# The last head's way to the output: normalised by two transposes, projected with the last tile

## Chip, core and metric

The kernel runs on one NeuronCore of a Trainium2 chip. The metric is the device time of one execution in microseconds (us). The engines are TensorE (PE in the profile; its weight loads are PEld), VectorE (DVE), ScalarE (ACT), GpSimd (POOL) and SyncE (SP, which here only issues DMAs).

## The reference

Two attention blocks of 32 heads with 18 columns each run over the same 2048 rows of `x` (576 columns), and a gate mixes them row by row:

```python
g = sigmoid((x * gate_w).sum(-1, keepdims=True))
a = A(x)    # o = softmax(q k^T / sqrt(18)) v, each head with its own k and v; then o @ A_wo
b = B(x)    # the same, but all heads share one k and one v; then o @ B_wo
return g * a + (1 - g) * b
```

`A_wo` and `B_wo` are 576 x 576. The kernel treats the job as 64 heads: 0 to 31 are those of B, 32 to 63 those of A. Their outputs, scaled by the gate and by one over the softmax sum, stand one below the other as 1152 rows, and the result is one product of these rows, transposed, with the 1152 rows of both output matrices.

## The kernel before

A first stage (lines 95 to 434) projects `x`. Then one loop (from line 799) goes through 1024 steps, 16 for each of the 64 heads, two at a time; T counts steps, a pass of the loop is a pair. In a step, TensorE makes the scores of 128 keys against all 2048 queries (`step_scores`, L550, four matmuls), ACT takes four exponentials (L557), and TensorE adds the product with the values into `acc`, one PSUM bank that holds a head's sum (`step_pv`, L563). 22 steps ahead, `step_max` finds row maxima for a later head: matmuls L513, reductions on VectorE L522 and L519, one relu per pair on ACT, L516.

The order within a pair is written out by hand in strings (lines 791 to 797). UNIT is used in a pair that has an output unit, PLAIN in one that has none, END and AFTER around a head's end, ALONE from T = 1002, when no maxima are left to find. `s` is a score, `m` a maximum, `P`, `Q`, `h`, `H` and the like products with the values (P and Q whole, h and H half the columns), `U` an output unit.

When a head is done, `head_out` copies `acc` to SBUF (L573) and DMAs its 18 rows into a tile `ot` of 128 rows, and its softmax sums to DRAM. When the 128 rows of a tile are complete, `normalise` loads the sums and the gate, takes the reciprocal times the gate (L601, L602), writes it to DRAM, reads it back spread over rows as `R`, multiplies, and splits the result into a high and a low float32r part. It is a generator; the list `slow` holds such generators, and the loop takes one step of it per pair (two where T > 1000, none where (T + 22) is a multiple of 16).

The output projection (`out_proj`) goes in three segments of the 1152 rows: tiles 0 to 3, tiles 4 to 7, and tile 8. Each has 32 units (16 row blocks of the output times two halves of 288 columns). A unit is three matmuls for each tile (high times high, and the two mixed products; L679) and one addition into `oacc` on VectorE (L687). So a unit of the second segment has 12 matmuls, one of the third 3. `SEG` (line 771) gives for each segment when its weights are prepared, and between which steps its units are due: 942 to 1008 for the second, 1021 to 1034 for the third, so that 12 units of the third run in the loop and the other 20 behind it.

Tile 8 holds rows 1024 to 1151. Its first 110 belong to heads 56 to 62. They are normalised at T = 1010 at once (`run(normalise(8, at_end=True))`, multiplications and splits on VectorE, L619, L123, L125), into two tiles `end` that stay in SBUF. The last 18 rows belong to head 63, which is done only when the loop ends. `last_out` treats it by itself: it copies `acc` (L708), splits it (L121, L125), stacks high, high and low parts by 12 DMAs into `stk`, and gets the 2048 factors as columns `rl` by four transposes (L720), a reciprocal (L722) and a product with the gate (L724). The remaining units of the third segment run; then 32 matmuls with 54 rows (L730) multiply the stack with the last 18 rows of the weights (high, low, high), and VectorE scales each by `rl` and adds it to `oacc` (L733). After both halves of a row block SP stores its 288 KB.

PSUM has eight banks here: three `ps`, four `pm` and `acc`.

Of the kernel before, what the change touches and what calls it, by code (L numbers as in the profile page):

```python
# [14 lines left out]
OP = mybir.AluOpType  # L15
# [34 lines left out]
def gated_mix_kernel(ctx: ExitStack, tc: tile.TileContext, xT, wall, wv, wo, out):  # L50
# [3 lines left out]
    def dma(o, i, eng=None):  # L54
        o, i = (x.bitcast(F32) if x.dtype == F32R else x for x in (o, i))
        return (eng or nc.sync).dma_start(o, i)  # L56
# [62 lines left out]
    def split(src, h, l, eng_h, eng_l):  # L119
        if eng_h is nc.scalar:  # L120
            nc.scalar.activation(h, src, AF.Copy)  # L121
        else:
            eng_h.tensor_copy(h, src)  # L123
        if l is not None:
            eng_l.tensor_tensor(l, src, h.bitcast(F32), op=OP.subtract)  # L125
# [463 lines left out]
    def normalise(t, at_end=False):  # L589

        u0 = 0 if t == 0 else last_head(t - 1) + 1
        u1 = min(last_head(t) + 1, NU - 1)
        rows = min(P, DH * (NU - 1) - P * t)
        n = (u1 - u0) * 16
        sm = L["work"].tile([P, P], F32, name="sm", bufs=1)
        dma(sm[:n, :], sum_d[u0:u1, :].rearrange("h (s f) -> (h s) f", f=P))
        gt = L["work"].tile([P, P], F32, name="gt", bufs=1)
        dma(gt[:n, :], gu_d[u0:u1, :].rearrange("h (s f) -> (h s) f", f=P))
        yield
        yield  # L600
        nc.vector.reciprocal(sm[:n, :], sm[:n, :])  # L601
# [12 lines left out]
        yield  # L614
        if at_end:
            L["end"] = {y: L["pool"].tile([P, S], F32R, name=f"end{y}") for y in "hl"}
            for c in range(4):
                cs = slice(512 * c, 512 * c + 512)
                nc.vector.tensor_tensor(ot[:rows, cs], ot[:rows, cs], R[:rows, cs], op=OP.mult)  # L619
                split(ot[:rows, cs], L["end"]["h"][:rows, cs], L["end"]["l"][:rows, cs], nc.vector, nc.vector)  # L620
            return
        for c in range(4):
            cs = slice(512 * c, 512 * c + 512)
            h = L["work"].tile([P, 512], F32R, name="oh", bufs=1)
            l = L["work"].tile([P, 512], F32R, name="ol", bufs=1)
            nc.gpsimd.tensor_tensor(ot[:rows, cs], ot[:rows, cs], R[:rows, cs], op=OP.mult)
            yield
            split(ot[:rows, cs], h[:rows], l[:rows], nc.gpsimd, nc.gpsimd)
            yield
            yield  # L630
            dma(on_d[0][P * t:P * t + rows, cs], h[:rows])
            dma(on_d[1][P * t:P * t + rows, cs], l[:rows])
            yield
# [15 lines left out]
    def out_proj(t0, rows, first=False):  # L649

        nt = len(rows)
        oacc = L["oacc"]
        O = {}

        def load(q):
            for x, y in enumerate("hl"):
                if "end" in L:
                    O[q, y] = L["end"][y][:, 256 * q:256 * q + 256].rearrange("p (t s) -> p t s", t=1)
                    continue
                t = L["pool"].tile([P, nt, 256], F32R, name=f"oi{y}", bufs=2)  # L660
                dma(t, on_d[x][P * t0:P * (t0 + nt), 256 * q:256 * q + 256]
                    .rearrange("(t p) s -> p t s", p=P))
                O[q, y] = t

        load(0)
        yield
        w = WO[t0]
        for q in range(8):
            if q < 7:
                load(q + 1)  # L670
            o = {y: O[q, y] for y in "hl"}
            for s2 in range(2):
                st_ = 2 * q + s2
                for hf in range(2):
                    fp = ps_m.tile([P, 512], F32, name="pm")
                    n = 0
                    for a, b in PRODS:
                        for t, r in enumerate(rows):
                            nc.tensor.matmul(fp[:, 0:288], o[b][:r, t, s2 * P:(s2 + 1) * P],  # L679
                                             w[a][:r, t, 288 * hf:288 * hf + 288],  # L680
                                             start=(n == 0), stop=(n == 3 * nt - 1))
                            n += 1
                    dst = oacc[:, st_, 288 * hf:288 * hf + 288]
                    if first:
                        nc.scalar.activation(dst, fp[:, 0:288], AF.Copy)
                    else:
                        nc.vector.tensor_tensor(dst, fp[:, 0:288], dst, op=OP.add)  # L687
                    yield


    def prep_last():
        p2 = L["pool"]
        r0 = DH * (NU - 1)
        st = p2.tile([64, D], F32, name="wlst", tag="wost")
        L["wl"] = p2.tile([64, D], F32R, name="wl")
        l = p2.tile([64, D], F32R, name="wll", tag="wlst2")
        for i in range(3):
            dma(st[18 * i:18 * i + 18, :], wo[r0:r0 + 18, :])
        L["g"] = p2.tile([P, 16], F32, name="gl")
        dma(L["g"], g_d[1].rearrange("(s p) -> p s", p=P))  # L700
        yield
        split(st[:54], L["wl"][:54], l[:54], nc.gpsimd, nc.gpsimd)
        yield
        dma(L["wl"][18:36, :], l[18:36, :])

    def last_out():
        oe = L["work"].tile([P, 512], F32, name="oe", bufs=1)
        nc.scalar.activation(oe, acc, AF.Copy)  # L708
        oh = L["work"].tile([P, 512], F32R, name="oh", bufs=1)
        ol = L["work"].tile([P, 512], F32R, name="ol", bufs=1)  # L710
        split(oe, oh, ol, nc.scalar, nc.vector)
        stk = L["pool"].tile([64, S], F32R, name="stk")
        for j in range(4):
            cs = slice(512 * j, 512 * j + 512)
            dma(stk[0:18, cs], oh[32 * j:32 * j + 18, :])
            dma(stk[18:36, cs], oh[32 * j:32 * j + 18, :])
            dma(stk[36:54, cs], ol[32 * j:32 * j + 18, :])
        pt = ps_m.tile([P, 512], F32, name="pm")
        for c in range(4):
            nc.tensor.transpose(pt[:, P * c:P * c + P], oe[:, P * c:P * c + P], ident)  # L720
        r = L["work"].tile([P, 16], F32, name="rl")
        nc.vector.reciprocal(r.rearrange("p (j c) -> p c j", c=4),  # L722
                             pt.rearrange("p (c j d) -> p c j d", c=4, d=32)[:, :, :, 18])
        nc.vector.tensor_tensor(r, r, L["g"], op=OP.mult)  # L724
        oacc = L["oacc"]
        yield
        for st_ in range(16):
            for hf in range(2):
                ps = ps_m.tile([P, 512], F32, name="pm")
                nc.tensor.matmul(ps[:, 0:288], stk[0:54, st_ * P:st_ * P + P],  # L730
                                 L["wl"][0:54, 288 * hf:288 * hf + 288], start=True, stop=True)
                dst = oacc[:, st_, 288 * hf:288 * hf + 288]
                nc.vector.scalar_tensor_tensor(dst, ps[:, 0:288], r[:, st_:st_ + 1], dst,  # L733
                                               op0=OP.mult, op1=OP.add)
            dma(out[st_ * P:(st_ + 1) * P, :], oacc[:, st_, :])


    NSTEP = 16 * NU
# [28 lines left out]
    slow = [gates()]  # L767
    for t in range(8):
        when(16 * (last_head(t) + 1) + 3, lambda t=t: slow.append(normalise(t)))
    when(16 * (NU - 1) + 2, lambda: run(normalise(8, at_end=True)))  # L770
    SEG = ((0, [P] * 4, 450, 521, 857), (4, [P] * 4, 862, 942, 1008), (8, [DH * (NU - 1) - 8 * P], 950, 1021, 1034))
    for t0, rows, Ta, Tb, Tc in SEG:
        when(Ta, lambda t0=t0, rows=rows: slow.append(prep_wo(t0, rows)))
        when(Tb - 4, lambda t0=t0, rows=rows: (todo.append(out_proj(t0, rows, first=t0 == 0)), pull(1)))
    when(980, lambda: slow.append(prep_last()))


# [63 lines left out]
                        slow.pop(0)  # L841
    while slow:
        run(slow.pop(0))
    tail = last_out()
    next(tail)
    pull(10 ** 9)
    run(tail)


# [32 lines left out]
```

## Time and profile before

| | |
|---|---|
| median of 3 runs | 2694.31 us (2694.18 to 2694.47) |
| the profiled execution | 2694.18 us |
| its span (first to last instruction) | 2692.4 us |
| TensorE busy | 2658.4 us, 99% |
| VectorE busy | 2428.6 us, 90% |
| ACT busy | 2389.0 us, 89% |
| mean granted TensorE clock | 0.997 |

Busy time counts overlapping instructions of an engine once. Matmuls are pipelined and their ends are modelled, so a busy TensorE is not one at its peak. In lists of instructions the first number is the start in us from the span's start, the second the length of the stretch, then engine, line, operation, output and inputs, shapes and the count; in brackets stands how long the engine had been idle before and what ended it. The chain of waits is followed back from the last instruction; each of its lines is a start, a length and what the end waited for there.

### The profile page before, as it was taken

The numbers are of one execution on the slowest core, as the hardware profiler recorded it, in microseconds if no ns is written. First come the engines' busy times: TensorE is split into PE (matmuls) and PEld (weight loads), VectorE is DVE, ScalarE is ACT, GpSimd is POOL, SyncE is SP. The second block draws the span as 40 slices with busy tenths as digits, with TensorE's granted clock in tenths as the row PEclk, the third lists the DMA queues.
The fourth block names the chain that finished last, engine by engine and source line by source line (L and its number), as shares of the span: only waits on it lengthen the run. The fifth ranks groups of instructions, "written<-read, shape, count | busy, mean of one in ns | idle before, by whom it ended". The sixth has DMA issues, their size and how long they took to land.

```text
span 2692.4 us, 57950 instructions
## 1 busy us (share of the span) xinstructions
PE 2658.4 (99%) x22210; PEld 956.5 (36%) x22210; DVE 2428.6 (90%) x4616; ACT 2389.0 (89%) x4810; POOL 280.1 (10%) x520
## 2 busy tenths in 40 slices
PE   9999999999999999999999999999999999999999
PEld 6878322222222222222223333333333332223444
DVE  8347999999999999999999999999999999998865
ACT  4341899999999999999999999999999999998875
POOL 4740000002001100100110002000200011011000
PEclk9999999999999999999999999999999999999998
DMA  6332000011001100210132112112121212122312
GB/s 200 124 111 76 23 20 20 20 34 42 28 17 46 44 20 18 53 32 20 36 76 82 51 43 85 42 50 65 55 67 50 59 50 60 39 76 81 88 36 96
DMA packets 127089, 150.36 MB, mean 56 GB/s; under 512 B 55339, under 2 KB 94411, under 8 KB 125614
## 3 DMA queue, kind: packets, MB, share of 16 engines
q1 hardware_dynamic: 113628, 121.86, 16.0%
q0 software_dynamic: 7968, 19.23, 2.1%
q10 hardware_dynamic: 5216, 5.57, 0.6%
q8 instruction: 174, 2.85, 0.4%
q14 instruction: 103, 0.84, 0.1%
HBM read 90.89 MB, written 46.45 MB: 51 GB/s over the span
## 4 chain that ended last, share of the span: by engine, by line
ACT 53%; PE 35%; DVE 6%; DMA 2%; issue 2%; SPq 1%; POOL 0%; DVEq 0%; ACTq 0%; POOLq 0%
ACT pt L557 47%; PE acc L563 12%; PE ps L550 11%; ACT xb L516 6%; PE pm L679 4%; DVE mx L522 3%; PE pm L243 3%; PE ps L243 2%; PE ps L292 2%; PE pm L513 1%; SPq L56 1%; DVE oe L573 1%; DVE junk L519 1%; DMA oih<-onh 1%; DMA R<-r_d 1%
## 5 line engine op out<-in xcount | busy, mean ns | idle before, releaser
L557 ACT ACTIVATE pt<-ps 128x512 f32<-128x512 f32 x4052 | 2093.8, 639 | 64.6 <-PE pm L513 57.9
L522 DVE TENSOR_REDUCE mx<-pm 128x1 f32<-128x512 f32 x3094 | 1939.1, 682 | 86.9 <-PE pm L513 71.1
L550 PE MATMUL ps<-qs,ksb 56*128 56x512 f16 x2688 | 816.6, 379 | 12.0 <-ACT pt L557 0.6
L513 PE MATMUL pm<-ksb,qs 54*128 54x512 f16 x2363 | 737.2, 382 | 1.2 <-DVE mx L522 0.4
L563 PE MATMUL acc<-pt,vb 128*19 128x512 f32 (+1 forms) x6136 | 591.3, 457 | 1.9
L563 PE MATMUL acc<-pt,vg 128*19 128x256 f32 (+1 forms) x5664 | 579.5, 481 | 2.3 <-DVE oe L573 0.5
L513 PEld LDWEIGHTS <-qs 54*128 54x128 f16 x4096 | 330.5, 93 | 252.1 <-issue 195.3
L550 PE MATMUL ps<-qs,ksa 56*128 56x512 f16 x1364 | 404.4, 379 | 4.8 <-ACT pt L557 1.3
L550 PEld LDWEIGHTS <-ksb 56*128 56x128 f16 x2688 | 174.9, 94 | 616.2 <-issue 569.9
L513 PE MATMUL pm<-ksa,qs 54*128 54x512 f16 x1232 | 384.8, 382 | 0.6 <-ACT xb L516 0.4
L519 DVE CUSTOM_DVE_ANT_0 junk<-pm,xb 128x512 bf16<-128x512 f32 x501 | 340.5, 680 | 0.1
L516 ACT ACTIVATE xb<-pm 128x512 f32<-128x512 f32 x501 | 318.2, 635 | 0.4 <-PE pm L513 0.4
L550 PEld LDWEIGHTS <-ksa 56*128 56x128 f16 x1408 | 89.3, 94 | 328.8 <-issue 297.7
L532 POOL TENSOR_SCALAR mt<-mt 128x32 f32<-128x32 f32 x64 | 18.5, 288 | 1606.2 <-DVE mt L530 1606.2
L563 PEld LDWEIGHTS acc<-pt,vb 128*19 128x19 f32 x6136 | 103.9, 96 | 221.7 <-issue 204.6
L563 PEld LDWEIGHTS acc<-pt,vg 128*19 128x19 f32 x5664 | 96.0, 97 | 222.9 <-issue 205.0
L513 PE MATMUL pm<-kdb,qs 54*128 54x512 f16 x373 | 141.7, 380 | 0.0
L573 DVE COPY oe<-acc 128x512 f32<-128x512 f32 x63 | 43.6, 692 | 30.0 <-PE acc L563 26.9
L295 ACT ACTIVATE vst<-ps 128x288 f32<-128x288 f32 x32 | 13.1, 411 | 62.9 <-PE ps L292 62.9
L251 ACT ACTIVATE ph<-ps,tv 128x512 f16<-128x512 f32 x29 | 19.8, 686 | 50.4 <-PE ps L243 34.3
L251 ACT ACTIVATE ph<-pm,tv 128x512 f16<-128x512 f32 x27 | 18.4, 686 | 48.4 <-PE pm L243 35.7
L257 DVE SCALAR_TENSOR_TENSOR pl<-pm,tv,ph 128x512 f16<-128x512 f32 x27 | 20.1, 749 | 37.9 <-ACT ph L251 24.9
(150 smaller groups left out, 1505.5 us busy)
## 6 DMA issues: line engine op xcount, KB each, us to landing
qs<-qkh SPq DMA_DIRECT2D x244, 72.0 KB
qs<-qkl SPq DMA_DIRECT2D x122, 72.0 KB
onh<-oh SPq DMA_DIRECT2D x32, 256.0 KB
onl<-ol SPq DMA_DIRECT2D x32, 256.0 KB
oih<-onh SPq DMA_DIRECT2D x16, 512.0 KB
oil<-onl SPq DMA_DIRECT2D x16, 512.0 KB
ot<-oe SPq DMA_DIRECT2D x220, 36.0 KB
R<-r_d SPq DMA_DIRECT2D x55, 144.0 KB
```

Of the source, the lines that this page charges most:

```text
L243: nc.tensor.matmul(fp[:, a0:b0], w[a][:kr, k, :], X[b][:kr, k, s0 + a0:s0 + b0], start=(n == 0), stop=(n == len(PROJ) - 1), skip_group_che ...
L251: nc.scalar.activation(h, fp, AF.Copy, scale=t)
L292: nc.tensor.matmul(fp[:, 0:288], X[b][:kr, k, st_ * P:(st_ + 1) * P], w[a][:kr, k, :], start=(n == 0), stop=(n == len(PROJ) - 1))
L513: nc.tensor.matmul(pm, qs[u % 3][b:b + 54, i * P:(i + 1) * P], k, start=True, stop=True)
L516: nc.scalar.activation(MX["x", u, i], pm, AF.Relu)
L519: nc.vector.tensor_tensor_reduce(junk, pm, MX.pop(("x", u, i)), 1.0, -3e38, op0=OP.add, op1=OP.max, accum_out=MX[u][:, i, c:c + 1])
L522: nc.vector.tensor_reduce(MX[u][:, i, c:c + 1], pm, axis=AX.X, op=OP.max)
L550: nc.tensor.matmul(ps, kst(u)[b:b + 56, i * P:(i + 1) * P], qs[u % 3][b:b + 56, c * 512:(c + 1) * 512], start=True, stop=True)
L557: nc.scalar.activation(pt, ps, AF.Exp, scale=SCALE / LIFT ** 2)
L563: nc.tensor.matmul(acc[32 * j:32 * j + 19, a:b], v_of(u, i), PT[u, i, j][:, a:b], start=(i == 0 and a == 0), stop=(i == 15), skip_group_ch ...
L573: nc.vector.tensor_copy(oe, acc)
L679: nc.tensor.matmul(fp[:, 0:288], o[b][:r, t, s2 * P:(s2 + 1) * P], w[a][:r, t, 288 * hf:288 * hf + 288], start=(n == 0), stop=(n == 3 * nt ...
```

## The change

- The last head is normalised in SBUF. `acc` is copied by two engines, ACT the left half of its columns, VectorE the right. Four transposes turn it, VectorE takes the reciprocals, multiplies with the gate, and multiplies the turned head with the factors (a product of 512 columns, read from PSUM). Four transposes turn it back; ACT and VectorE split it; eight DMAs, four from SP and four from ACT, put the 18 rows under the 110 in the `end` tiles.
- Tile 8 is then projected with 128 rows: 32 units of three matmuls, all behind the loop, and a plain addition. The third segment's units are gone from the loop, and so are the 54-row matmuls, their 12 DMAs and their weights. The units use seven PSUM banks, and the stores are issued by SP and ACT in turn.
- Five idle matmuls (54 rows, 512 columns, into `acc`) stand between the two groups of transposes, 14 behind the second.
- The first 110 rows are normalised through `slow`, with one more stop ahead of each of the four column blocks.
- The second segment's units are due until step 1016 instead of 1008.

```diff
             for c in range(4):
                 cs = slice(512 * c, 512 * c + 512)
+                yield
                 nc.vector.tensor_tensor(ot[:rows, cs], ot[:rows, cs], R[:rows, cs], op=OP.mult)
...
+    def end_bank(n=[0]):
+        n[0] += 1
+        return ps_s.tile([P, 512], F32, name="ps") if n[0] % 7 < 3 else ps_m.tile([P, 512], F32, name="pm")
...
+        def idle(n):
+            for _ in range(n):
+                nc.tensor.matmul(acc, qs[0][0:54, 0:P], qs[0][0:54, 0:512], start=True, stop=True)
+
+        nc.scalar.activation(oe[:, 0:256], acc[:, 0:256], AF.Copy)
+        nc.vector.tensor_copy(oe[:, 256:512], acc[:, 256:512])
+        pt, pb = end_bank(), end_bank()
         for c in range(4):
             nc.tensor.transpose(pt[:, P * c:P * c + P], oe[:, P * c:P * c + P], ident)
+        idle(5)
...
+        nc.vector.reciprocal(r.rearrange("p (j c) -> p c j", c=4), p4[:, :, :, DH])
         nc.vector.tensor_tensor(r, r, L["g"], op=OP.mult)
+        nc.vector.tensor_tensor(o4, p4, r.rearrange("p (j c) -> p c j", c=4).unsqueeze(3).to_broadcast([P, 4, 4, 32]),
+                                op=OP.mult)
+        for c in range(4):
+            nc.tensor.transpose(pb[:, P * c:P * c + P], ot[:, P * c:P * c + P], ident)
+        idle(14)
+        nc.scalar.activation(oh, pb, AF.Copy)
+        nc.vector.tensor_tensor(ol, pb, oh.bitcast(F32), op=OP.subtract)
+        r0 = DH * (NU - 1) - 8 * P
+        for j in range(4):
+            dma(end["h"][r0:P, 512 * j:512 * j + 512], oh[32 * j:32 * j + DH, :])
+            dma(end["l"][r0:P, 512 * j:512 * j + 512], ol[32 * j:32 * j + DH, :], nc.scalar)
+        w = WO[8]
         for st_ in range(16):
             for hf in range(2):
+                fp = end_bank()
+                for n, (a, b) in enumerate(PRODS):
+                    nc.tensor.matmul(fp[:, 0:288], end[b][:, st_ * P:(st_ + 1) * P],
+                                     w[a][:, 0, 288 * hf:288 * hf + 288], start=(n == 0), stop=(n == 2))
+                dst = L["oacc"][:, st_, 288 * hf:288 * hf + 288]
+                nc.vector.tensor_tensor(dst, fp[:, 0:288], dst, op=OP.add)
+            dma(out[st_ * P:(st_ + 1) * P, :], L["oacc"][:, st_, :], nc.scalar if st_ % 2 else None)
...
-    when(16 * (NU - 1) + 2, lambda: run(normalise(8, at_end=True)))
-    SEG = ((0, [P] * 4, 450, 521, 857), (4, [P] * 4, 862, 942, 1008), (8, [DH * (NU - 1) - 8 * P], 950, 1021, 1034))
+    when(16 * (NU - 1) + 2, lambda: slow.append(normalise(8, at_end=True)))
+    SEG = ((0, [P] * 4, 450, 521, 857), (4, [P] * 4, 862, 942, 1016))
...
+    when(950, lambda: slow.append(prep_wo(8, [P])))
...
-    tail = last_out()
-    next(tail)
     pull(10 ** 9)
-    run(tail)
+    last_out()
```

More of the change, by code (lines that the diff above doesn't have):

```diff
@@ L656, in load @@
             for x, y in enumerate("hl"):
-                if "end" in L:
-                    O[q, y] = L["end"][y][:, 256 * q:256 * q + 256].rearrange("p (t s) -> p t s", t=1)
-                    continue
                 t = L["pool"].tile([P, nt, 256], F32R, name=f"oi{y}", bufs=2)
@@ L691, in prep_last @@
     def prep_last():
[L692 to L699, printed above, removed]
+        L["g"] = L["pool"].tile([P, 16], F32, name="gl")
         dma(L["g"], g_d[1].rearrange("(s p) -> p s", p=P))
@@ L701, in prep_last @@
         yield
-        split(st[:54], L["wl"][:54], l[:54], nc.gpsimd, nc.gpsimd)
-        yield
-        dma(L["wl"][18:36, :], l[18:36, :])
+    def end_bank(n=[0]):
+        n[0] += 1
+        return ps_s.tile([P, 512], F32, name="ps") if n[0] % 7 < 3 else ps_m.tile([P, 512], F32, name="pm")
     def last_out():
[L707 to L718, printed above, removed]
+        oe, ot = (L["work"].tile([P, 512], F32, name=x, bufs=1) for x in ("oe", "oT"))
+        oh, ol = (L["work"].tile([P, 512], F32R, name=x, bufs=1) for x in ("oh", "ol"))
@@ L719, in last_out @@
+        end = L["end"]
+        def idle(n):
[4 more added lines that the diff above has]
+        pt, pb = end_bank(), end_bank()
         for c in range(4):
             nc.tensor.transpose(pt[:, P * c:P * c + P], oe[:, P * c:P * c + P], ident)
+        idle(5)
         r = L["work"].tile([P, 16], F32, name="rl")
-        nc.vector.reciprocal(r.rearrange("p (j c) -> p c j", c=4),
-                             pt.rearrange("p (c j d) -> p c j d", c=4, d=32)[:, :, :, 18])
+        p4, o4 = (x.rearrange("p (c j d) -> p c j d", c=4, d=32) for x in (pt, ot))
@@ L724, in last_out @@
+        nc.vector.reciprocal(r.rearrange("p (j c) -> p c j", c=4), p4[:, :, :, DH])
         nc.vector.tensor_tensor(r, r, L["g"], op=OP.mult)
-        oacc = L["oacc"]
-        yield
+        nc.vector.tensor_tensor(o4, p4, r.rearrange("p (j c) -> p c j", c=4).unsqueeze(3).to_broadcast([P, 4, 4, 32]),
[4 more added lines that the diff above has]
+        nc.scalar.activation(oh, pb, AF.Copy)
@@ L727, in last_out @@
+        nc.vector.tensor_tensor(ol, pb, oh.bitcast(F32), op=OP.subtract)
[4 more added lines that the diff above has]
+        w = WO[8]
         for st_ in range(16):
             for hf in range(2):
-                ps = ps_m.tile([P, 512], F32, name="pm")
-                nc.tensor.matmul(ps[:, 0:288], stk[0:54, st_ * P:st_ * P + P],
-                                 L["wl"][0:54, 288 * hf:288 * hf + 288], start=True, stop=True)
@@ L732, in last_out @@
[L732 to L735, printed above, removed]
+                fp = end_bank()
+                for n, (a, b) in enumerate(PRODS):
+                    nc.tensor.matmul(fp[:, 0:288], end[b][:, st_ * P:(st_ + 1) * P],
+                                     w[a][:, 0, 288 * hf:288 * hf + 288], start=(n == 0), stop=(n == 2))
```

## The prediction

> **What bounds the kernel now.** I read the page first, then the chain of waits over the last 90 us, and then the timelines of single engines inside that stretch. The profiled execution took 2694.18 us, its span 2692.4, so 1.8 lie around it.
>
> ```profile
> span 2692.4 us, 57950 instructions
> ```
>
> All sums below are made against this execution; the median of the three runs is 0.13 higher.
>
> The chain in order of time (start, length, what), one pair of steps after the other:
>
> ```profile
> 2602.95 1.80 PE pm L679 x12
> ...
> 2605.07 0.21 PE ps L550
> ...
> 2608.76 1.78 PE pm L679 x12
> ...
> 2613.37 1.80 PE pm L679 x12
> ...
> 2615.71 0.56 PE acc L563 x8
> ...
> 2617.47 0.98 PE acc L563 x8
> ...
> 2618.45 1.78 PE pm L679 x12
> ...
> 2639.08 0.32 PE pm L550 x2
> ...
> 2643.00 0.32 PE pm L550 x2
> ```
>
> L679 x12 is one unit of the second segment, 1.8 us of TensorE. In the order UNIT a pair that has one lasts 2608.76 - 2602.95 = 5.81, and the chain there is TensorE alone. In the order ALONE (from step 1002, no maxima left) a pair with a unit lasts 2618.45 - 2613.37 = 5.08, also all TensorE. An ALONE pair with no unit lasts 2643.00 - 2639.08 = 3.92, with ACT's exponentials in the chain.
>
> ACT's timeline just before the second segment's first unit:
>
> ```profile
> 2434.11 0.65 ACT L516 ACTIVATE xb<-pm 128x512 f32<-128x512 f32 x1
> 2434.59 4.18 ACT L557 ACTIVATE pt<-ps 128x512 f32<-128x512 f32 x8
> 2438.61 0.65 ACT L516 ACTIVATE xb<-pm 128x512 f32<-128x512 f32 x1
> 2439.09 4.09 ACT L557 ACTIVATE pt<-ps 128x512 f32<-128x512 f32 x8
> 2443.05 0.61 ACT L516 ACTIVATE xb<-pm 128x512 f32<-128x512 f32 x1
> ```
>
> A pair with no unit lasts 2438.61 - 2434.11 = 4.50 and 2443.05 - 2438.61 = 4.44, and ACT has no gap: nine operations at 0.49. So a unit there costs 5.81 - 4.44 = 1.37, not its 1.8 of TensorE, of which 0.43 was slack.
>
> The end of the loop and the tail, from the timelines of ACT, PE, DVE and the DMA queue:
>
> ```profile
> 2651.66 1.63 ACT L557 ACTIVATE pt<-pm 128x512 f32<-128x512 f32 x2
> ...
> 2660.25 1.08 ACT L557 ACTIVATE pt<-ps 128x512 f32<-128x512 f32 x2 [0.33 <-PE ps L550]
> ```
>
> ```profile
> 2664.77 0.63 PE L563 MATMUL acc<-pt,vg 128*19 128x256 f32 x8
> ...
> 2665.70 0.29 PE L679 MATMUL pm<-wol,endh 110*128 110x288 f32 x1
> 2665.83 0.29 PE L679 MATMUL pm<-woh,endh 110*128 110x288 f32 x1
> ...
> 2666.23 0.60 PE L720 MATMUL pm<-ident,oe 128*128 128x128 f32 x4
> ...
> 2674.85 3.78 PE L730 MATMUL pm<-wl,stk 54*128 54x288 f32 x10
> ```
>
> ```profile
> 2666.11 0.48 PEld L720 LDWEIGHTS pm<-ident,oe 128*128 128x128 f32 x4
> ```
>
> ```profile
> 2665.46 0.60 ACT L708 ACTIVATE oe<-acc 128x512 f32<-128x512 f32 x1 [4.12 <-PE acc L563]
> ```
>
> ```profile
> 2666.82 0.69 DVE L125 TENSOR_TENSOR ol<-oe,oh 128x512 fp32r<-128x512 f32 x1
> 2667.43 0.25 DVE L722 RECIPROCAL rl<-pm 128x16 f32<-128x16 f32 x1
> 2667.71 0.18 DVE L724 TENSOR_TENSOR rl<-rl,gl 128x16 f32<-128x16 f32 x1
> 2667.81 7.61 DVE L687 TENSOR_TENSOR oacc<-pm,oacc 128x288 f32<-128x288 f32 x20
> 2675.33 13.68 DVE L733 SCALAR_TENSOR_TENSOR oacc<-pm,rl,oacc 128x288 f32<-128x288 f32 x32
> ```
>
> Call E the end of the last head's sum: 2664.77 + 0.63 = 2665.40. From E to the span's end are 27.0 us, and VectorE fills most of them: 20 adds of the third segment at 0.38, then 32 adds of the last head at 13.68/32 = 0.43, until 2689.0; 3.4 more for the last store and the close. ACT had finished its last exponential at 2661.33; TensorE held E up by 4 us with units of the third segment.
>
> **The change, part by part.**
>
> *Second segment to step 1016.* By the formula in `due` 25 units instead of 29 fall before step 1002 and 7 instead of 3 behind it; the pairs that lose theirs (956, 970, 986, 1000) stand alone. Each saves at least that 1.37. TensorE's own work without the unit is 5.81 - 1.80 + 0.14 = 4.15 (in PLAIN the second product is two halves, 2 x 0.56 instead of 0.98), and for one pair three score banks let it run ahead of ACT, so at most 1.66. I take 1.55: -6.2 (-5.5 to -6.6). The four ALONE pairs 1008 to 1014 go from 3.92 to 5.08: +4.6, and +0.3 because pair 1010's first product waits for head 62's copy, a wait that ACT has covered so far: +4.9 (4.4 to 5.1). The adds of these units lie on a VectorE that has only head 62's copy and the last tile's work there.
>
> *Third segment out of the loop.* Twelve units leave the pairs from 1020 on. Then ACT ends last: its exponentials for the last two pairs start at 2651.66, 16 at 0.49 make 7.84, the last one's tail 0.12, and the two half products 2 x 0.56: E at 2660.8 instead of 2665.4, -4.6 (-4.0 to -4.8).
>
> *The last tile in pieces.*
>
> ```profile
> 2636.92 0.34 SPq L56 DMA_DIRECT2D sm<-sum_d  x1
> ```
>
> ```profile
> 2638.63 0.95 DVE L601 RECIPROCAL sm<-sm 96x128 f32<-96x128 f32 x1 [6.63 <-DMA sm<-sum_d]
> ...
> 2649.92 0.69 DVE L619 TENSOR_TENSOR ot<-ot,R 110x512 f32<-110x512 f32 x1 [10.01 <-DMA R<-r_d]
> ```
>
> Run at once, this generator would hold VectorE for 6.63 and 10.01 us in front of the adds of the units that now run in these pairs. In pieces the reciprocal stands behind pair 1012's add and the four column blocks behind 1016 and 1020. Behind the reciprocal only pair 1014's add waits. SP issues the same loads in the same order. The blocks are done some 6 us ahead of E (11.3 us from reciprocal to R, then 7.2 of VectorE). Cost nothing; if the reciprocal waited a pair longer, one PSUM bank of four would be held and TensorE would lose perhaps 1 us. The POOL split of the last head's weights goes from an engine with nothing late.
>
> *The tail, from E.* Half copies: ACT's 256 columns by its rows 0.60 (512) and 0.411 (288), VectorE's by 0.69 and 0.46:
>
> ```profile
> L573 DVE COPY oe<-acc 128x512 f32<-128x512 f32 x63 | 43.6, 692 | 30.0 <-PE acc L563 26.9
> L295 ACT ACTIVATE vst<-ps 128x288 f32<-128x288 f32 x32 | 13.1, 411 | 62.9 <-PE ps L292 62.9
> ```
>
> so 0.38 and 0.43. Do they run side by side? The first stage has a case: VectorE's L257 waits for ACT's L254, though both only read one bank (who waited for L254, us and times):
>
> ```profile
>   DVE pl L257: 23.8, 11
> ```
>
> I take them one behind the other, ready at E + 0.9 (side by side 0.5). The Trainium skill, "PSUM — Partial Sum Buffer", section "PSUM bank collisions raise a hardware error", says that two engines in one bank collide even on disjoint columns and that the compiler's scheduler puts such accesses in order; by it the half copies gain nothing over one copy of 0.60, without it the sum is 0.4 less. The trace's case reads the same columns twice, so it does not show disjoint ones.
>
> The first two transposes hide under VectorE's half; the other two, at half of the 0.72 that four take from first load to last product (2666.11 to 2666.83), end at 1.4. Reciprocal and product 0.46: 1.9. The 512-column product 0.69: 2.6. Four transposes: 3.4. ACT's copy 0.60: 4.0. VectorE's `ol` 0.69: 4.75. Then ACT issues the first `l` DMA. A load's landing, from rows: issue 2636.92, reciprocal 2638.63, so 1.7: 6.5. That load is from DRAM; the landing of a copy within SBUF is not shown, and I allow 0.5 either way. The h DMAs left SP 0.7 earlier. The other columns' DMAs follow at 0.7-0.8 each:
>
> ```profile
> 2666.81 1.53 SPq L56 DMA_DIRECT2D stk<-oh  x2
> ...
> 2675.47 0.72 SPq L56 DMA_DIRECT2D stk<-ol  x1
> 2676.31 13.06 SPq L56 DMA_DIRECT2D out<-oacc  x16
> ```
>
> while one set of columns feeds 3.1 us of products, so only the first pair is on the path. (L730 began at 2674.85, before the last `stk` DMA left at 2675.47, so products wait by columns, not for the tile.) The 14 idle matmuls are 14 x 0.21 = 3.0 on TensorE, ahead of the projection in its queue, 3.4 to 6.4: they hide behind the landing; the five hide behind VectorE's 1.15. Then 96 products at 2665.83 - 2665.70 = 0.13: 12.6, to 19.2; VectorE's plain add keeps up at 0.38 per 0.39, and seven banks instead of four smooth it. Last product and add 0.65: 19.9. Store and close 3.4: 23.3. The stores need 288 KB per 0.79 us, 373 GB/s, from two queues:
>
> ```profile
> 2677.20:2690.60 13.40, 10.77 (x25) 7.07 (x25) 11.82 (x28) 0.00 (x0) 0.00 (x0) 0.50 0.93 350
> ...
> 281.05:284.46 3.41, 2.82 (x18) 0.70 (x19) 3.29 (x7) 3.41 (x8) 0.00 (x0) 1.00 0.01 2
> ```
>
> (Windows: busy us of PE, its loads, DVE, ACT and POOL, then clock, DMA share, GB/s.) 350 GB/s took a DMA share of 0.93, so about 376 is the most: they fit barely, perhaps 0.5 late. Tail 23.3 instead of 27.0: -3.7 (-4.1 to -2.5).
>
> Sum: -6.2 + 4.9 - 4.6 - 3.7 = **-9.6, 2684.6 us**, -0.36%.
>
> **Rivals.** *Half clock for a window or two.* The granted clock (third number from the end in the last two rows) fell to 0.50 at 2677.2, 2 us after the dense products ended and L730 ran 0.13 in every 0.43, and stayed there. From 281.05 to 284.46, with 18 products in 3.41 us, it was 1.00. Between E and E + 3.4 the new tail has five idle matmuls, 1.1 us, and eight transposes. So this is near the line. If it falls there, the 14 idle ones take up to 6.0 instead of 3.0 and a few products follow at half rate: +1.5 (back at full rate within them) to +3.5, 2686.1 to 2688.1. The Trainium skill, "TensorE: Matmul & The Clock Gate", Parts 1 and 4, has windows of 3.4 us and says that transposes do not count as activity; by that a third of such a window (1.1 of 3.4) counts as active, and the time is the one just given. The fall at 2677.2 does not contradict it; no row here shows what transposes alone do to the clock.
>
> *Half clock to the end (slower).* If the clock stays at 0.50 as it did for the last 15 us, 14 idle and 96 products cost twice: 3.0 + 12.6 more, of which 0.1 hides: tail 38.8, total 2700.1. It turns slower than before once about 50 of the 96 run at half rate. Against it: the projection is dense, unlike L730.
>
> *The moves cancel.* If ACT and VectorE give the four lone pairs no slack (-5.5), the ALONE pairs cost 5.1, and TensorE's last products lag 0.6, E moves -5.5 + 5.1 - 4.0 = -4.4; a tail bound by the stores gives -2.5: 2687.3; and if the products wait for all eight DMAs (the last leaves 3 x 0.75 after the first, so lands at 8.7 instead of 6.5) 2.2 more, 2689.5, no measurable difference.
>
> **How the numbers follow.** Full clock as worked out 0.66; short half clock 0.15; cancelled 0.12, of which half within the bound; half clock to the end 0.06; 0.01 left. 0.2% is 5.4 us, about what a measurement of this kernel tells from no change: faster means under 2688.9. Faster 0.82, same 0.11, slower 0.07. Of the range, the low end takes the terms' bounds (-6.6 + 4.4 - 4.8 - 4.1 = -11.1, 2683.1), the high end the long short-half-clock case (2688.1) and the first cancelled one; 0.9 more on each side is for landings and waits that no row shows: 2682.2 to 2689.0.
>
> **What would show it.** ALONE pairs 1008 to 1014 at 5.1; lone pairs at 4.2; E near 2659.5; VectorE's half of `oe` starting after ACT's; first projection product at E + 6.5 and 32 adds at 0.39; the clock at 1.00 until the close. Wrong would be: a clock of 0.50 in the tail, a first product later than E + 7, stores that end over 3.4 after the last add, or lone pairs at 5.8.

## The result and the profile after

The changed kernel takes 2688.91 us (median of 17 runs, 2687.92 to 2692.19), the kernel before, run in turn with it, 2694.53 (17 runs). The ratio is 0.998, with an interval of 0.9973 to 0.9986, so the gain is 5.6 us by the medians: in the forecast direction, 4.0 less than the forecast 9.6, at the upper end of the range. The profiled execution of the changed kernel took 2688.88 us, 5.30 less than that of before. Of all runs below two took over 10300 us, one in the changed kernel's second series and one without the idle matmuls; the ratios leave them out. From the page after:

```profile
span 2687.1 us, 57952 instructions
...
PE 2650.9 (99%) x22233; PEld 952.1 (35%) x22233; DVE 2416.2 (90%) x4586; ACT 2387.9 (89%) x4810; POOL 278.8 (10%) x518
...
q8 instruction: 175, 2.87, 0.4%
```

1.8 us lie around the span, as before, so the two traces can be laid side by side. They differ by less than 0.2 us up to the first pair that loses its unit, and by 0.02 us there. ACT's relus (one per pair) at that place, before:

```profile
2477.87 0.60 ACT L516 ACTIVATE xb<-pm 128x512 f32<-128x512 f32 x1
...
2483.67 0.60 ACT L516 ACTIVATE xb<-pm 128x512 f32<-128x512 f32 x1
...
2489.47 0.60 ACT L516 ACTIVATE xb<-pm 128x512 f32<-128x512 f32 x1
```

and after:

```profile
2477.89 0.60 ACT L516 ACTIVATE xb<-pm 128x512 f32<-128x512 f32 x1
...
2480.18 2.55 ACT L557 ACTIVATE pt<-ps 128x512 f32<-128x512 f32 x5 [0.17 <-PE pm L513]
2482.59 0.64 ACT L516 ACTIVATE xb<-pm 128x512 f32<-128x512 f32 x1
2483.06 3.10 ACT L557 ACTIVATE pt<-ps 128x512 f32<-128x512 f32 x6
...
2488.25 0.60 ACT L516 ACTIVATE xb<-pm 128x512 f32<-128x512 f32 x1
```

Before, two pairs take 5.80 + 5.80. After, the lone pair takes 4.70 and the next one 5.66: together 1.24 less. The brackets, idle time ahead of a row, show why: from 2480.18 to 2486.16 ACT has no gap. With the unit gone ACT sets the pace from there on, not TensorE. TensorE's score matmuls after, the first of the lone pair, of the next and of the one behind, and between them two that stand side by side in the next pair:

```profile
2478.02 0.39 PE L550 MATMUL ps<-qs,ksa 56*128 56x512 f16 x1
...
2482.20 0.39 PE L550 MATMUL ps<-qs,ksa 56*128 56x512 f16 x1
...
2484.34 0.38 PE L550 MATMUL ps<-qs,ksa 56*128 56x512 f16 x1
...
2484.75 0.37 PE L550 MATMUL ps<-qs,ksa 56*128 56x512 f16 x1
...
2488.38 0.39 PE L550 MATMUL ps<-qs,ksa 56*128 56x512 f16 x1
```

On TensorE the lone pair takes 4.18, what its own work needs, and the next one 6.18 instead of 5.80: the wait for ACT falls into the pair behind. The two in its middle stand 0.41 apart, the same two of the lone pair 0.21 (2479.99 and 2480.20).

The chain of waits after, over the loop's end and the tail (start, length, what the end waited for):

```profile
2606.70 0.32 PE pm L550 x2
...
2608.01 1.80 PE pm L677 x12
...
2613.09 1.78 PE pm L677 x12
...
2627.11 0.70 DVE oe L573
...
2650.71 0.32 PE pm L550 x2
...
2657.99 3.13 PE acc L563 x32
...
2661.15 0.39 ACT oe L708
...
2661.59 0.44 PE ps L712 x2
...
2663.03 0.70 DVE oT L718
...
2664.53 0.61 ACT oh L723
...
2665.16 0.70 DVE ol L724
...
2665.88 2.52 DMA endl<-ol
...
2668.44 0.55 PE pm L734 x2
...
2669.01 12.76 DVE oacc L737 x32
```

and before, at the start of pair 1018:

```profile
2646.92 0.32 PE pm L550 x2
```

Before, the unit of pair 1002 began at 2613.37; now it begins at 2608.01, 5.36 earlier. Before, pair 1018 began at 2646.92 and an ALONE pair took 3.92, so pair 1020 began at 2650.84; now it begins at 2650.71. What the lone pairs won is spent again in the ALONE pairs. From there to E it is 10.4 us instead of 14.6: E is 2661.1 (2657.99 + 3.13), 4.3 earlier than the 2665.4 of before. The tail from E takes 26.0 instead of 27.0.

| term | forecast | measured in the two profiles |
|---|---|---|
| lone pairs | -6.2 | -5.36 |
| ALONE pairs 1002 to 1014 | +4.9 | +5.23 |
| third segment out of the loop | -4.6 | -4.16 |
| tail from E | -3.7 (23.3) | -0.99 (25.98) |
| sum | -9.6 | -5.28 |

In the tail two stretches are longer than forecast. The second product, the first that needs an `l` row, starts at E + 7.3 instead of 6.5. The last add ends at 2669.01 + 12.76 = 2681.77, E + 20.66 instead of 19.9, so what lies between is as forecast (12.76/32 = 0.40 an add). Then the close, from the issue of the last store just behind the last add to the end of the span, takes 5.3 instead of 3.4. The windows (busy us of PE, its loads, DVE, ACT, POOL, then clock, DMA share, GB/s) show the stores and what follows them:

```profile
2669.80:2683.70 13.90, 11.48 (x87) 11.24 (x85) 11.97 (x31) 0.00 (x0) 0.00 (x0) 1.00 0.91 342
2683.70:2685.54 1.84, 0.00 (x0) 0.00 (x0) 0.00 (x0) 0.00 (x0) 0.00 (x0) 0.53 0.07 26
2685.54:2687.10 1.56, 0.00 (x0) 0.00 (x0) 0.00 (x0) 0.00 (x0) 0.00 (x0) 0.50 0.00 0
```

For 1.84 us the DMA share is 0.07, about one engine of sixteen (0.0625): one DMA engine has not finished its part of the stores while fifteen stand idle. Before, the last 3.2 us (from 2689.2, in 40 equal slices, busy tenths of the DMA engines) end all at once:

```profile
DMA  9999899668899999964000000000000000000000
```

The DMA view over the 1.4 us from 2679.6, some 3 us ahead of it (kind of queue, packets, MB, share of 16 engines), after, shows what that engine may have done instead:

```profile
q8 instruction: 1, 0.02, 4.3%
q14 instruction: 1, 0.01, 1.4%
```

One packet of instructions, 4.3% of 16 engines over 1.4 us: 0.96 us of one engine. The page above has 175 such packets with 2.87 MB, 16 KB each. TensorE issued 22233 products and as many loads, 44466 instructions, and 44466/256 = 174: this is TensorE's own program, fetched 256 instructions at a time. The kernel before, and the two kernels below whose TensorE has 64 and 38 instructions fewer, have 174 packets. The Trainium skill, "Runtime: NRT & Kernel Launch", section "Instruction fetch mechanics", says that the sequencer refills its program in 16 KiB blocks of 256 instructions through a DMA queue of its own, and it calls the cost of crossing into the next block mostly hidden. The count agrees.

### The profile page after: what moved, and what is told of

Same layout as the page of the kernel before. It is cut to its first block, busy times and chain, and to the rows that moved or that the text cites. A ratio compares the mean times of both kernels' runs of the same rounds, so it can differ in the third digit from the quotient of the medians.

```text
span 2687.1 us, 57952 instructions
## 1 busy us (share of the span) xinstructions
PE 2650.9 (99%) x22233; PEld 952.1 (35%) x22233; DVE 2416.2 (90%) x4586; ACT 2387.9 (89%) x4810; POOL 278.8 (10%) x518
## 3 DMA queue, kind: packets, MB, share of 16 engines
q8 instruction: 175, 2.87, 0.4%
## 4 chain that ended last, share of the span: by engine, by line
ACT 54%; PE 37%; DVE 5%; DMA 1%; issue 1%; SPq 0%; POOL 0%; ACTq 0%; DVEq 0%; POOLq 0%
ACT pt L557 48%; PE acc L563 13%; PE ps L550 11%; ACT xb L516 6%; PE pm L677 4%; DVE mx L522 3%; PE pm L243 3%; PE ps L243 2%; PE ps L292 2%; PE pm L513 1%; DVE oe L573 1%; DVE junk L519 1%; DVE oacc L737 0%; DMA xs<-xT 0%; SPq L56 0%
## 5 line engine op out<-in xcount | busy, mean ns | idle before, releaser
L532 POOL TENSOR_SCALAR mt<-mt 128x32 f32<-128x32 f32 x64 | 18.6, 290 | 1631.3 <-DVE mt L530 1631.3
```

## The experiments

All are edits of the changed kernel; times are medians, ratios are to the kernel before on the same chip. The changed kernel, run again beside some of them, gave 2689.43 (10 runs), ratio 0.9975 [0.9966, 0.9985], E + 7.33 for the second product and a close of 4.79, with its own instruction packet at E + 18.6:

> The changed kernel itself again, on the chip of the next three, to have E, the close and the clock side by side. Expected: first product of the second group at E + 7.3, last store issued at E + 20.7, close 5.2 to 5.4 with the instruction packet at E + 18 to 19.

The close came out 0.4 to 0.6 shorter than expected: two executions of the same kernel differ by 0.5 in it, with the packet at the same place.

**The late close.** Theory F: the instruction packet holds one DMA engine up while the stores fill all sixteen. Rival S: the stores themselves, alternating from two queues, end late. The edit adds 104 products of 16 columns long before the end (each is overwritten by the real one), so that the fetch comes 208 instructions earlier and so ahead of the stores:

```diff
         pm = ps_m.tile([P, 512], F32, name="pm")
+        if c == 2 and i % 2 == 0 and 8 <= u < 21:
+            nc.tensor.matmul(pm[:, 0:16], qs[u % 3][b:b + 54, i * P:(i + 1) * P], k[:, 0:16], start=True, stop=True)
         nc.tensor.matmul(pm, qs[u % 3][b:b + 54, i * P:(i + 1) * P], k, start=True, stop=True)
```

> After, with 104 extra matmuls of 16 columns (one per pair, in heads 8 to 20, into a PSUM bank that the next matmul overwrites; the result is the same), 208 TensorE instructions more ahead of the tail. In the trace of after TensorE's instruction packets of 16 KB come once per 256 of its instructions, the last at 2679.91, in the middle of the stores; it held one DMA engine for 0.96 us, and one engine's last 16 store packets ended at 2685.5 while the others had ended at 2683.7. Theory F (the instruction packet makes one engine late): the packet moves ahead of the stores (to about 2665), the close from the last store's issue to the end of the span shrinks from 5.3 to 3.5-3.8, total 1.5 to 1.8 faster than after, about 2687.2. Rival S (the stores simply come faster than the DMA engines drain them): the close stays 5.0 to 5.3, total as after, 2688.9.

Measured: 2688.51, ratio 0.9975 [0.9965, 0.9985]. E to the second product and the adds are unchanged to 0.01 us; the close is 3.74 instead of 5.29. The DMA view from 2668.6 to 2670.2, E + 7.2 to 8.8, now has the packet, and behind the stores one engine runs on for 0.4 us instead of 1.8:

```profile
q8 instruction: 1, 0.02, 3.8%
```

```profile
2670.10:2683.75 13.65, 11.43 (x87) 11.20 (x85) 11.93 (x31) 0.00 (x0) 0.00 (x0) 1.00 0.93 350
2683.75:2684.16 0.41, 0.00 (x0) 0.00 (x0) 0.00 (x0) 0.00 (x0) 0.00 (x0) 1.00 0.06 23
2684.16:2685.80 1.64, 0.00 (x0) 0.00 (x0) 0.00 (x0) 0.00 (x0) 0.00 (x0) 0.72 0.00 0
```

Same stores, nearly the same rate, and the lone engine's stretch is down to 0.4 us: F holds, S falls. The other kind of packet (q14) still comes at E + 18.6 here, so it isn't the cause. Where page and trace differ: "mostly hidden" is true of TensorE, which waited for nothing, and not of the DMA engine that brings the block. Run once more, to see whether the gain in time is real:

> e1 again on the chip of the other two, as their standard: E to end 24.4, close 3.7.

Measured: 2688.15, ratio 0.9974 [0.9964, 0.9984], close 4.15 instead of the expected 3.7, E to end 24.8. The two medians lie 0.4 and 0.8 under the changed kernel's first one, 0.9 and 1.3 under its second; the intervals overlap. The mechanism is shown by the close, its worth in the median, about 1 us, only by direction. Over the profiles of all kernels with the full clock in the tail: with the packet at E + 17.7 to 18.8 the close is 4.61 to 5.29 and E to the end 25.3 to 26.0 (six profiles); with the packet ahead of the stores 3.65 to 4.15 and 24.4 to 24.8 (four). The one exception is the kernel with all eight DMAs on SP, below.

Is it the stores' second queue that makes the close sensitive (theory Q)? All stores from SP:

```diff
-            dma(out[st_ * P:(st_ + 1) * P, :], L["oacc"][:, st_, :], nc.scalar if st_ % 2 else None)
+            dma(out[st_ * P:(st_ + 1) * P, :], L["oacc"][:, st_, :])
```

> After, with all 16 stores issued by SP. Theory F (the instruction packet): nothing changes, close 5.2 to 5.4, total within 0.4 of after. Rival Q (two queues taken in turn by each DMA engine leave one of them behind): the close shrinks to 3.5 to 4.0 and the total by 1.3 to 1.8. By either, SP's issues of 0.35 fit into the 0.79 between stores.

Measured: 2689.43, ratio 0.9978 [0.9969, 0.9987], close 4.61 with a packet of 1.45 us at E + 17.7. F's 5.2 to 5.4 did not come, but 4.61 lies near the 4.79 of the changed kernel's second series, and there is no gain in time. Q's 3.5 to 4.0 did not come either, so Q is not borne out, and a second queue isn't needed for the stores.

**The second segment's move alone.**

```diff
-    SEG = ((0, [P] * 4, 450, 521, 857), (4, [P] * 4, 862, 942, 1016))
+    SEG = ((0, [P] * 4, 450, 521, 857), (4, [P] * 4, 862, 942, 1008))
```

> After, with the second segment's units due until step 1008 again. Theory (units cost as much in the ALONE pairs as in the others; by the traces the move brought -5.35 ahead of step 1002 and +5.23 behind it): within 0.3 of after up to E, total within 0.5 of after. Rival (the prediction's step: four lone pairs save 1.55 each, four ALONE pairs cost 1.16 each): 1.3 slower than after. The last instruction packet stays where it is, since the number of instructions is the same: close 5.3.

Measured: 2688.24, ratio 0.9974 [0.9964, 0.9984]. From a mark ahead of the moved units to E it is 0.18 us more than in the changed kernel: that is all the move is worth, where the prediction's terms gave 1.3. What I had wrong is that the number of TensorE's instructions would stay: a pair in PLAIN has its second product in halves, so there are 32 products (64 instructions) fewer. The packet that the changed kernel has at E + 0.1 came at E + 7.5, the one among the stores was not fetched, and the close was 3.70. So this kernel confirms F a second time, without meaning to, and it is no slower than the changed one.

**The idle matmuls.** Theory C: they keep the clock up and are worth some us; the rival: they are not needed, since eight transposes and the products do it.

```diff
-        idle(5)
...
-        idle(14)
```

> After, without the 19 idle matmuls. Theory C (they keep the granted clock up): the clock falls to 0.50 one 3.41 us window after E or two, some 10 to 20 us before after's does, and 20 to 60 of the 96 products run at twice the length: 3 to 8 slower than after. Rival N (the transposes and the short wait are not enough to lower the clock): total as after or up to 1.7 faster, because 38 instructions fewer push the last instruction packet past the end of TensorE's program and the close shrinks to 3.5-3.8.

Measured: 2691.14, ratio 0.9983 [0.9974, 0.9992]. The windows:

```profile
2662.82:2665.81 2.99, 1.21 (x8) 0.73 (x8) 1.55 (x4) 0.38 (x1) 0.00 (x0) 1.00 0.01 3
2665.81:2676.05 10.24, 6.81 (x29) 6.12 (x27) 3.90 (x8) 0.60 (x1) 0.00 (x0) 0.50 0.27 86
2676.05:2689.71 13.66, 9.67 (x73) 9.44 (x72) 9.98 (x25) 0.00 (x0) 0.00 (x0) 1.00 0.80 303
```

The clock falls 3.0 us after E (here 2662.82) and stays at 0.50 for 10.24 us, though the dense products run from E + 7.5. VectorE's adds are 0.72 apart there instead of 0.40, and the last add ends at E + 23.40 instead of 20.66: 2.7 us. C holds for the clock, but the cost is under the 3 to 8 us expected: 38 instructions fewer also took the packet from among the stores, the close is 3.71, and from E to the end it is 27.1 instead of 26.0. The median is 1.7 to 2.2 over the two series of the changed kernel, and not all of that is the edit's: this execution also shows a clock of 0.50 from 283.31 to 286.72, just behind the first stage, where the edit changes nothing, and 1.0 us is lost there. The profile of the run with all eight DMAs on SP, below, has the same at 283.02; how many runs had it, the traces don't show. The Trainium skill, "TensorE: Matmul & The Clock Gate", Part 1, has free-running windows of 3.413 us; 10.24 is three of them, so the trace agrees in the length.

**The late second product.** In the changed kernel the queues of SP and ACT read:

```profile
2665.15 3.02 SPq L56 DMA_DIRECT2D endh<-oh  x4
```

```profile
2665.88 3.95 ACTq L56 DMA_DIRECT2D endl<-ol  x4
```

Four issues took SP 3.02 and ACT 3.95; ACT's first alone took 1.65. Theory A: it is ACT's first DMA after a long pause, and cold. Rival D: two engines that issue at once share something. A's test has ACT issue an earlier load, of the gate's column:

```diff
-        dma(L["g"], g_d[1].rearrange("(s p) -> p s", p=P))
+        dma(L["g"], g_d[1].rearrange("(s p) -> p s", p=P), nc.scalar)
```

> After, with the load of the last gate column (step 980) issued by ACT instead of SP, so that the first low-part DMA of the tail is not ACT's first DMA since the first stage (279 us). In after that DMA's issue took 1.64 us, ACT's next three 0.72 to 0.75. Theory A (a first issue after a long time is slow): its issue takes 0.7 to 0.8, the products wait until E + 6.5 instead of 7.3, total 0.8 faster than after. Rival D (it shares something with SP's issues, which run at the same time): 1.6 again, total as after.

Measured: 2689.28, ratio 0.9978 [0.9969, 0.9987]; the first issue still 1.64, the second product at E + 7.33. A falls, at least for an issue 115 us ahead. Then the first `l` DMA from SP, the other three from ACT:

```diff
-            dma(end["l"][r0:P, 512 * j:512 * j + 512], ol[32 * j:32 * j + DH, :], nc.scalar)
+            dma(end["l"][r0:P, 512 * j:512 * j + 512], ol[32 * j:32 * j + DH, :], nc.scalar if j else None)
```

> After, with the low part's first DMA issued by SP right behind the high part's first; the other three low DMAs stay with ACT. Both theories of the 1.64 us: its issue takes 0.7-0.8 on SP from E + 4.85, it lands at E + 6.6, the products start 0.7 earlier than after's, the last store leaves at E + 20.0 instead of 20.7, total 0.6 to 0.8 faster. Theory A: ACT's own first DMA now takes 1.6 and lands before its columns are due at E + 9.8, so nothing waits. If the store packets bind instead of the products, the gain is lost in the close.

Measured: 2689.67, ratio 0.9979 [0.9971, 0.9988]; the second product at E + 7.34, nothing won of the expected 0.6 to 0.8. The issue on SP took 0.73, but its packets left 1.68 us after its start, behind those of ACT's. The miss spoke for D, so the next kernel takes ACT out altogether: all eight from SP (and the 104 products, to have the fetch out of the way):

```diff
-            dma(end["l"][r0:P, 512 * j:512 * j + 512], ol[32 * j:32 * j + DH, :], nc.scalar)
+            dma(end["l"][r0:P, 512 * j:512 * j + 512], ol[32 * j:32 * j + DH, :])
```

> e1 (instruction packet ahead of the stores) with all eight DMAs of the two parts issued by SP in turn, high, low, high, low, and none by ACT. Theory D (the two queues share what makes the packets: in after ACT's first took 1.64 to issue beside SP's, in e6 SP's own low part left 1.68 instead of 1.40 after its issue because ACT's had gone ahead): the low part's issue takes 0.7 from E + 4.8, its packets leave 1.40 after that and have landed at 6.55, the second group starts at E + 6.95 instead of 7.33, the last store leaves at E + 20.3, close 3.7, 0.4 faster than e1. Rival (a copy within SBUF takes this long to be seen, whoever issues it): 7.3 as in after and e6.

Measured: 2689.56, ratio 0.9978 [0.9969, 0.9987]. The chain's wait for the `l` rows, then SP's queue (E is 2662.60):

```profile
2667.50 2.08 DMA endl<-ol
...
2669.62 0.54 PE pm L736 x2
```

```profile
2666.64 0.76 SPq L56 DMA_DIRECT2D endh<-oh  x1
2667.50 0.73 SPq L56 DMA_DIRECT2D endl<-ol  x1
...
2671.98 0.70 SPq L56 DMA_DIRECT2D endl<-ol  x1
2672.78 9.73 SPq L56 DMA_DIRECT2D out<-oacc  x8
```

2.08 instead of 2.52, and the second product at E + 7.0 instead of 7.3: D holds, sharing costs 0.4. What the two issues share isn't shown. But SP is busy with the eight until E + 10.1, the first store's packets leave 0.6 later, at E + 10.2, and the close is 4.80 though the packet came ahead of the stores, at E + 7.5. Here the stores' rate is the limit, which the expectation had not counted: from 2672.85 to 2685.40 the DMA share is 1.00 at 377 GB/s. From E to the end it is 25.2 us, against 24.4 and 24.8 with the 104 products alone, so more is lost at the end than was won at the front. The Trainium skill, "DMA: Bandwidth & Descriptors", section "Issuing engines are not separate DMA queues", says that a second issuing engine saves only the time of issuing. Here it did not even save all of that: one issue beside the other engine's took 1.65 instead of 0.7.

The pieces put together (the 104 products, the first `l` DMA from SP, four idle matmuls during the half copies):

```diff
+        for _ in range(4):
+            nc.tensor.matmul(pb, qs[0][0:54, 0:P], qs[0][0:54, 0:512], start=True, stop=True)
```

> After with three edits: the 104 small matmuls of e1 (instruction packet ahead of the stores), the low part's first DMA on SP as in e6, and four more idle matmuls of 512 columns into the second transposes' bank while the half copies run (E to E + 0.9, behind nothing). If the terms add: close 3.7 instead of 5.3 (-1.6), products 0.7 earlier, so 2.0 to 2.4 faster than after in runs of full clock, E + 23.6 in all, about 0.9966 of before. Rival: the stores are then at the rate of the DMA engines and the close takes back the 0.7: 1.5 faster. With the four idle matmuls fewer runs should show a clock of 0.998 (after had 3 of 17).

Measured: 2688.86, ratio 0.9975 [0.9965, 0.9985]. The close is 3.65, but the transposes wait behind the four matmuls, everything after is 0.2 to 0.4 later, and nothing is won over the 104 products alone: the terms did not add. None of its 9 runs has a clock of 0.998, too few to say that the four matmuls did it.

**The last tile in pieces.** Forecast as free; what would it have cost at once?

```diff
-    when(16 * (NU - 1) + 2, lambda: slow.append(normalise(8, at_end=True)))
+    when(16 * (NU - 1) + 2, lambda: run(normalise(8, at_end=True)))
```

> After, with the last tile's 110 rows normalised at once at step 1010, as before. Theory V (VectorE is held by the two waits, 6.6 and 10 us, ahead of the additions of the units that now run in pairs 1010 to 1014; a unit's PSUM bank stays taken, and the four banks are also those of the scores): TensorE stops until the blocks are done, 18.6 + 7.2 us after head 62's sum instead of some 6: E 10 to 20 later, total 10 to 20 slower than after. Rival (the additions only wait and the banks suffice): within 1 of after.

Measured: 2712.86 (4 runs), ratio 1.0064 [1.0051, 1.0078], slower than before the change. VectorE's timeline, and the windows:

```profile
2634.98 0.95 DVE L601 RECIPROCAL sm<-sm 96x128 f32<-96x128 f32 x1 [6.77 <-DMA sm<-sum_d]
...
2645.97 0.69 DVE L620 TENSOR_TENSOR ot<-ot,R 110x512 f32<-110x512 f32 x1 [9.72 <-DMA R<-r_d]
...
2653.13 1.18 DVE L685 TENSOR_TENSOR oacc<-pm,oacc 128x288 f32<-128x288 f32 x3
```

```profile
2639.00:2644.76 5.76, 4.14 (x33) 2.01 (x32) 0.00 (x0) 3.46 (x8) 0.00 (x0) 1.00 0.57 141
2644.76:2685.70 40.94, 33.02 (x170) 4.60 (x162) 8.07 (x15) 19.33 (x35) 0.00 (x0) 0.50 0.00 1
```

VectorE waits 9.72 us for `R`, three adds stand behind it until 2653.13, TensorE is busy 4.14 of 5.76 us, and the clock falls to 0.50 for 41 us, the rest of the loop. VectorE has caught up at 2654.3, but the pairs stay long. The chain shows one of them:

```profile
2657.11 0.58 PE pm L550
...
2666.12 0.58 PE pm L550
```

A pair takes 9.0 us instead of 3.9, so the 41 us hold 4.6 pairs and lose 4.6 x 5.1 = 23 us. I had expected 10 to 20 us, from TensorE standing still; from a mark ahead of step 1010 to E it is 24.5 more. The standing still is the small part, the clock the large one.

## Why the prediction was right and wrong

The profile lacks 4.3 us of the forecast gain. The step that failed most is the store and close, taken over from before as 3.4 us (1.9 too short); then come the lone pairs and the landing of the `l` rows (0.8 each), and 0.8 in two terms that were nearly right. That 2688.9 us still lies under the range's upper end of 2689.0 is luck: that end was taken from the half clock, which the profile of the changed kernel doesn't show, and 0.9 for landings and waits.

*Right.* What bounds the kernel, the ALONE pairs (5.08 each, +5.2 with the copy of head 62 in the chain, forecast +4.9), the loop's end (-4.2 for -4.6, inside its bounds), both within 0.4 of the forecast, and every step of the tail from E to `ol`: forecast E + 4.75, measured 2665.86 - 2661.12 = 4.74. The half copies do run one behind the other: VectorE's began 0.04 after the end of ACT's 0.39. The second half's transposes end at E + 1.38; one copy by ACT (0.60) and four transposes (0.72) would end at about 1.4, an estimate from the prediction's rows, so the two halves gain nothing. The order shows for disjoint columns what the prediction's row showed for the same ones; the rule of the Trainium skill that it cites from "PSUM — Partial Sum Buffer" agrees. The clock stayed at 1.00 until 2683.8, behind the last product, and the run without idle matmuls shows how near the half-clock rival was. Three of the 17 runs, with a mean clock of 0.998 where the others have 0.999 or 1.000, took 2691.3 to 2692.2; that would fit this rival's short case, but also a fall just behind the first stage, such as the run without idle matmuls had at 283.31; no trace of such a run was taken. The tail's sum up to the last add missed only by the landing. The 376 GB/s estimated as the most for the stores is what the run with all eight DMAs on SP shows (377 at a DMA share of 1.00).

*Wrong by 0.8: a lone pair saves 1.55.* A lone pair saves 1.24 in the three places where another UNIT pair follows, under both bounds that I gave (1.37 and 1.66). That TensorE runs ahead of ACT for the one pair is right: the lone pair takes it 4.18, as the 4.2 named as a sign. What failed is that I did not count the pair behind. ACT is late by then and has no gap until 2486.16, TensorE waits for it, and that pair takes 6.18 instead of 5.80, so 0.4 of the 1.66 are lost again, where I had taken off 0.11. Only the last lone pair, with the ALONE order behind it, gives more: 5.36 - 3 x 1.24 = 1.6.

*Wrong by 0.8: the landing of the l rows.* I took 1.7 from a load from DRAM, counted from its issue to the instruction that waited for it. Counted the same way the copy within SBUF took 2.52. Of the 0.8 more, 0.4 come from SP issuing at the same time, as the run with all eight on SP shows (2.08). The other 0.4 are the remainder; what in the copy takes them is not shown.

*Wrong by 1.9: store and close 3.4.* The step took the close of before as fixed. Before, its last instruction packet came ahead of the stores. Now TensorE's instructions are counted otherwise, and a block falls among the last stores, which need 0.9 of the DMA engines: one engine is held for 0.96 us by it, and its part of the stores ends 1.84 after the others'. I had the DMA share in hand and asked only whether the bandwidth would do on the average, not what else would come to one of the engines. With the packet out of the way the close was 3.7 and 4.15 in two runs of the same kernel, so 1.1 to 1.6 of the 1.9 are the packet's, and the rest is not explained.

*The rival "the moves cancel"* described the loop best: it had E at -4.4, and -4.3 was measured. Its reason for the tail, the bandwidth of the stores, was not the one found in the changed kernel; it showed only where the stores began later, in the run with all eight on SP. My chance of 0.82 for a gain over 0.2% gave too little to a sum of small misses that all go the same way: -5.6 lies just at that bound.

Still open: why ACT's issue beside SP's takes 1.65 (what the two share isn't in the trace), why one engine ends 1.8 late where the packet took 1.0, and why the close differs between 3.7 and 4.2 with the packet out of the way.

## What to carry to other kernels

Before a unit of work is moved out of a pair, look at the pair behind it as well: a single short step between long ones saves less than the same step in a row of short ones. Count the end of a kernel by its slowest DMA engine, not by the mean rate: where stores fill all sixteen, one 16 KB block of TensorE's program on one of them shows in the close, and any change in the number of TensorE's instructions moves that block, so a difference of about 1 us can come from nothing that the edit was meant to do. Idle matmuls across a DMA wait were worth 2.7 us at the last add here, and a stalled VectorE cost most through the clock.

## What the runs showed of the hardware that was not expected

- TensorE's program comes in packets of 16 KB, one for 256 instructions (175 packets for 44466 products and loads). Around the tail one took 0.88 to 1.56 us of one DMA engine. One among stores that fill all sixteen engines made the close 0.5 to 1.6 us longer.
- Of two DMAs issued at once by SP and ACT, one issue took 1.65 us instead of 0.7; with all on SP the rows landed 0.4 sooner.
- With 8 transposes and no other product in 3.0 us the clock fell to 0.50. It stayed there for 10.24 us, three stretches of 3.41, with TensorE busy for 0.52, 2.88 and all of them, and was back behind the full one. With VectorE stalled it stayed at 0.50 for 41 us, twelve such stretches, while TensorE was busy for 33 of the 41.
